# Routed attention and a cosine router: attention with keys on partitions and two heads per matmul slot

## The chip, the cores and the metric

One core of a Trainium2 chip runs the whole program. The metric is device time in microseconds of one execution. Before: 1521.6 us, the median of 3 runs (1513.58 to 1528.15).

## The reference

Attention runs on 4 batches, 8 heads, 768 tokens of 64 numbers. Each query and each key goes to the nearest of its head's 16 centroids by cosine, and a query sees only keys of its own cluster. The result, 3072 tokens of 512 numbers, goes through a router that sends each token to one of 8 experts.

```python
# attention: q, k, v (4, 8, 768, 64), centroids (8, 16, 64)
q_assign = argmax(einsum('bhsd,hcd->bhsc', q_n, c_n), axis=-1)      # *_n: rows of unit length
k_assign = argmax(einsum('bhsd,hcd->bhsc', k_n, c_n), axis=-1)
mask = q_assign[:, :, :, None] == k_assign[:, :, None, :]
scores = where(mask, scale * q @ k^T, -1e9)
scores = scores - max(scores, axis=-1)
attn = exp(scores);  attn = attn / (sum(attn, -1) + 1e-9)
x = attn @ v                                                        # to (3072, 512)
# router: 8 experts, 512 -> 1024 -> 512
idx, gate = argmax and softmax weight of cosine(x, expert_emb) / tau
out = gate * (relu(x @ w1[idx]) @ w2[idx])
```

All inputs and the output are fp32. A query without any key of its cluster has equal scores everywhere, so its row of x is the mean of v.

## The kernel before

The program has four stages in one stream: constants and a first preparation, attention with the routing of finished batches in between, the sorting of tokens by expert ("places"), and 31 blocks of 128 tokens through the experts. The change is in the first two.

Attention goes over 16 pairs of heads (4 batches with 4 pairs each). A pair has the two heads side by side: q and k are turned so that partitions 0 to 63 hold the numbers of the first head and 64 to 127 those of the second. A unit is one tile of 128 queries of one head, 6 tiles per head, 12 units per pair, 192 in all. Three units make a group, half a head, 64 groups in all.

What a unit does, by name and line:

- `scores` (L289): TensorE writes a 128 x 768 block, queries on partitions and all keys as columns, into two PSUM banks. Two bf16 matmuls (L296) multiply one-hot clusters so that keys of other clusters get a huge negative number; two fp32 matmuls, four instructions in the trace (L304), add q times k. Each uses the 64 partitions of its head. VectorE then finds the negated row maximum (L312).
- `expo` (L314): ScalarE takes the exponential with that maximum as bias and sums each row on the way (L320).
- `turn_probs` (L328): six TensorE transposes (L338) turn the probabilities so that keys lie on partitions; VectorE copies one half out of PSUM (L344), ScalarE the other (L346).
- `attend` (L349): for the group before, two key blocks per loop are multiplied with v into a 64 x 384 block (L356); after six blocks ScalarE copies it out (L365).
- `finish` (L367): for a group two back, three transposes (L373) turn the output, and VectorE divides by the row sums (L376, L377, L381) into `xr`, the rows of x of a batch.

Preparation of the next pair (`prep_pieces`, L200) is cut into nine pieces, one per loop: four times three transposes of q or k (L211) with a copy, the products with the centroids as 12 matmuls of 128 tokens against 32 columns (L227, `assign`), the choice of the first greatest product (VectorE and GpSimd), and the turning of the one-hot clusters (L259). Pieces, finish and routing share one PSUM bank, `misc`. Routing of a finished batch (`route_pieces`, L389) is cut into eight pieces in the same way.

The order on TensorE, VectorE and ScalarE is the written order of the main loop (L467): scores of unit i+1, finish, transposes of unit i, exponential of unit i+1, a piece of preparation, a third of attend, a piece of routing. Loads of q, k and v (`load`, L116) are issued on SyncE's queue and wait for a buffer, of which there are two of each.

Of the kernel before, what the change touches and what calls it, by code (L numbers as in the profile page):

```python
# [9 lines left out]
F32 = mybir.dt.float32  # L10
# [11 lines left out]
BIG = 2.0**60  # L22
# Adding and subtracting it rounds to an integer.
CMAGIC = 12582912.0
# Index of rows that hold no token: out of bounds, so they are not written.
# [8 lines left out]
def kernel(  # L34
# [31 lines left out]
    # Rows of x by token, each with the token's gate behind it.  # L66
# [13 lines left out]
    prefe = const.tile([P, E], BF16, name="prefe")  # L80
    io_i = const.tile([P, P], I32, name="io_i")
# [16 lines left out]
    # ================= attention and routing =================  # L98
    with ExitStack() as at:
# [39 lines left out]
        nc.vector.memset(onesb, 1.0)  # L139
        nc.vector.memset(cnB, 0.0)  # L140
# [9 lines left out]
        # Slot s = b * NJ + j holds token b * S + p * NJ + j on partition p.  # L150
# [10 lines left out]
        # One-hot clusters, 64 columns per head: those of the centroids, then -1 for q and 1 for k.  # L161
        ohs = [const.tile([P, 2, NJ, 2, D], BF16, name=f"oh{i}") for i in range(2)]
        for oh in ohs:
            nc.gpsimd.memset(oh, 0.0)
            for t in range(2):
                nc.gpsimd.memset(oh[:, t, :, :, C : C + 1], (-1.0, 1.0)[t])
# [33 lines left out]
        def prep_pieces(n):  # L200
            """Turned q (scaled) and k of a pair of heads, and their turned one-hot clusters."""
# [19 lines left out]

            def assign():
                bk = misc()
                for i, nm in enumerate("qk"):
                    for j in range(NJ):
                        c0 = 2 * C * (NJ * i + j)
                        nc.tensor.matmul(  # L227
                            bk[:, c0 : c0 + 2 * C],
                            lhsT=t[nm + "T"][:, P * j : P * j + P],
                            rhs=cnB[:, hp],  # L230
                            start=True,
                            stop=True,
                        )
# [9 lines left out]
            def choose():  # L243
                """One-hot clusters: the first of those with the greatest product."""
# [4 lines left out]
                    oh.rearrange("p t j h c -> p (t j h) c")[:, :, 0:C],  # L249
# [5 lines left out]
            def turn_hot(i, nm):  # L255
                hot = t[nm + "H"] = trp.tile([P, S], BF16, tag=nm + "H", name=nm + "H")
                bk = misc().bitcast(BF16)
                for j in range(NJ):
                    nc.tensor.transpose(  # L259
                        bk[:, P * j : P * j + P],  # L260
                        oh[:, i, j].rearrange("p h c -> p (h c)"),
# [6 lines left out]

            return [
                lambda: turn("q", 0),  # L270
                lambda: turn("k", 0),
                lambda: turn("q", 1),
                lambda: turn("k", 1),
                assign,
                None,
# [5 lines left out]
        # Units of attention: a tile of queries of one head; in groups of three, half a head.  # L281
        units = [(n, h, j) for n in range(len(pairs)) for h in range(2) for j in range(NJ)]
        GU = NJ // 2
# [5 lines left out]
        def scores(i):  # L289
            n, h, j = units[i]  # L290
            t = ld[n]
            rows = slice(D * h, D * h + D)
            s_ps = un[i]["s_ps"] = psS.tile([P, 1024], F32, tag="s_ps", name="s_ps")
            # The clusters first: between equal ones their sum is 0, and the scores stay exact.
            for lo, hi in ((0, 512), (512, S)):
                nc.tensor.matmul(  # L296
                    s_ps[:, lo:hi],
                    lhsT=t["qH"][rows, P * j : P * j + P],
                    rhs=t["kH"][rows, lo:hi],
                    start=True,  # L300
                    stop=False,
                )
            for lo, hi in ((0, 512), (512, S)):
                nc.tensor.matmul(  # L304
                    s_ps[:, lo:hi],
                    lhsT=t["qT"][rows, P * j : P * j + P],
                    rhs=t["kT"][rows, lo:hi],
                    start=False,
                    stop=True,
                )  # L310
            nmax = un[i]["nmax"] = smp.tile([P, 1], F32, tag="nmax", name="nmax", bufs=4)
            nc.vector.tensor_reduce(nmax, s_ps[:, 0:S], axis=AXX, op=ALU.max, negate=True)  # L312

        def expo(i):  # L314
            d = un[i]
            g, u = divmod(i, GU)
            if u == 0:
                gr[g]["den"] = smp.tile([P, GU], F32, tag="den", name="den", bufs=4)
            d["prob"] = pp.tile([P, S], F32, tag="prob", name="prob", bufs=3)
            nc.scalar.activation(  # L320
                d["prob"],
                d["s_ps"][:, 0:S],
                ACTF.Exp,
                bias=d["nmax"],
                accum_out=gr[g]["den"][:, u : u + 1],
            )

        def turn_probs(i):  # L328
            d = un[i]
            g, u = divmod(i, GU)  # L330
            if u == 0:
                gr[g]["pT"] = pp.tile([P, NJ, HS], F32, tag="pT", name="pT", bufs=2)
            pT = gr[g]["pT"]
            for half in range(2):
                t_ps = psT.tile([P, HS], F32, tag="t_ps", name="t_ps")
                for c in range(GU):
                    c0 = HS * half + P * c
                    nc.tensor.transpose(  # L338
                        t_ps[:, P * c : P * c + P], d["prob"][:, c0 : c0 + P], ident
                    )  # L340
                dst = pT[:, GU * half : GU * half + GU, P * u : P * u + P]
                src = t_ps.rearrange("p (c m) -> p c m", m=P)
                if half == 0:
                    nc.vector.tensor_copy(dst, src)  # L344
                else:
                    nc.scalar.copy(dst, src)  # L346
            d.clear()

        def attend(g, part):  # L349
# [405 lines left out]
```

## Time and profile before

| | |
|---|---|
| median of 3 runs | 1521.6 us (1513.58 to 1528.15) |
| span of the profiled execution | 1522.6 us |
| its own time beside the span | not given apart from the span |
| mean granted TensorE clock | 0.956 |
| busy: TensorE, VectorE, ScalarE, GpSimd | 1426.1, 469.1, 407.1, 117.0 us |

The span runs from the first to the last instruction of one execution. "Busy" is the time in which an engine works on an instruction; for TensorE, matmuls overlap in the records, so the time from one start to the next says more than a duration. A releaser in square brackets behind a row names what ended the engine's idle time before it. The granted clock is the share of full speed that TensorE was given; its levels are 1.2 and 2.4 GHz. In the first 50 us the column shows 1.00 although matmuls take twice their later time there. A timeline merges like instructions that follow each other; x4 is four of them.

### The profile page before, as it was taken

The numbers are of one execution on the slowest core, as the hardware profiler recorded it, in microseconds if no ns is written. First come the engines' busy times: TensorE is split into PE (matmuls) and PEld (weight loads), VectorE is DVE, ScalarE is ACT, GpSimd is POOL, SyncE is SP. The second block draws the span as 40 slices with busy tenths as digits, with TensorE's granted clock in tenths as the row PEclk, the third lists the DMA queues.
The fourth block names the chain that finished last, engine by engine and source line by source line (L and its number), as shares of the span: only waits on it lengthen the run. The fifth ranks groups of instructions, "written<-read, shape, count | busy, mean of one in ns | idle before, by whom it ended". The sixth has DMA issues, their size and how long they took to land.

```text
span 1522.6 us, 14912 instructions
## 1 busy us (share of the span) xinstructions
PE 1426.1 (94%) x5715; PEld 749.9 (49%) x5715; DVE 469.1 (31%) x925; ACT 407.1 (27%) x830; POOL 117.0 (8%) x153
## 2 busy tenths in 40 slices
PE   5999999989999998999998999957999999999997
PEld 3544554545455554555554555443444444444443
DVE  2434444333344333444443344432111111111110
ACT  2333333332333323333333333310111111111110
POOL 1000000000000010000000000021111111111110
PEclk9999999878999978999998999957999999999999
DMA  9110110101101101011011000000726575534310
GB/s 285 41 32 0 32 32 1 31 27 47 27 6 32 32 1 63 11 32 32 1 32 42 11 11 1 1 41 22 257 85 254 194 257 196 198 143 146 137 39 0
DMA packets 106134, 107.73 MB, mean 71 GB/s; under 512 B 77445, under 2 KB 77445, under 8 KB 105552
## 3 DMA queue, kind: packets, MB, share of 16 engines
q1 hardware_dynamic: 100928, 92.30, 19.0%
q0 software_dynamic: 4960, 14.44, 2.6%
q8 instruction: 45, 0.74, 0.2%
q14 instruction: 25, 0.20, 0.0%
q10 hardware_dynamic: 176, 0.05, 0.0%
HBM read 165.48 MB, written 14.43 MB: 118 GB/s over the span
## 4 chain that ended last, share of the span: by engine, by line
PE 60%; issue 20%; DMA 12%; DVE 4%; ACT 2%; POOL 0%; POOLq 0%; ACTq 0%; DVEq 0%
PE o_ps L356 19%; PE s_ps L304 17%; DMA out_dram<-y,sidx 12%; PE t_ps L338 9%; PE s_ps L296 6%; PE misc L227 3%; PE misc L211 2%; PE misc L411 2%; DVE nmax L312 2%; PE misc L401 1%; ACT xT L405 1%; PE misc L259 1%; DVE xr L381 1%; DVE den L377 0%; PE misc L373 0%
## 5 line engine op out<-in xcount | busy, mean ns | idle before, releaser
L312 DVE TENSOR_REDUCE nmax<-s_ps 128x1 f32<-128x768 f32 x192 | 183.8, 957 | 459.3 <-PE s_ps L304 459.3
L356 PE MATMUL o_ps<-pT,v 128*64 128x384 f32 x768 | 305.3, 523 | 0.0
L304 PE MATMUL s_ps<-kT,qT 64*128 64x512 f32 (+1 forms) x768 | 294.5, 506 | 0.0
L346 ACT COPY pT<-t_ps 128x384 f32<-128x384 f32 x192 | 91.7, 478 | 580.8 <-PE t_ps L338 580.8
L656 PE MATMUL h_ps<-w1s,xTm 128*128 128x512 f32 x496 | 222.2, 601 | 0.0
L679 PE MATMUL y_ps<-w2s,hT 128*128 128x512 f32 x496 | 218.7, 593 | 1.2 <-DVE hT L673 1.2
L304 PEld LDWEIGHTS s_ps<-kT,qT 64*128 64x128 f32 x768 | 135.1, 196 | 118.9 <-issue 95.4
L338 PE MATMUL t_ps<-ident,prob 128*128 128x128 f32 x1152 | 177.9, 293 | 0.0
L320 ACT ACTIVATE prob<-s_ps,nmax 128x768 f32<-128x768 f32 x192 | 173.9, 906 | 7.0 <-DVE den L376 3.7
L338 PEld LDWEIGHTS t_ps<-ident,prob 128*128 128x128 f32 x1152 | 130.2, 147 | 60.1 <-issue 57.4
L679 PEld LDWEIGHTS y_ps<-w2s,hT 128*128 128x128 f32 x496 | 93.9, 190 | 118.6 <-issue 116.7
L356 PEld LDWEIGHTS o_ps<-pT,v 128*64 128x64 f32 x768 | 93.6, 142 | 108.7 <-issue 104.9
L656 PEld LDWEIGHTS h_ps<-w1s,xTm 128*128 128x128 f32 x496 | 92.6, 191 | 110.2 <-issue 106.2
L648 DVE COPY xTm<-x_ps 128x512 f32<-128x512 f32 x31 | 21.4, 691 | 389.7 <-PE x_ps L646 389.7
L344 DVE COPY pT<-t_ps 128x384 f32<-128x384 f32 x192 | 105.2, 548 | 1.4 <-PE t_ps L338 1.3
L663 ACT ACTIVATE h<-h_ps 128x512 f32<-128x512 f32 x62 | 37.0, 597 | 248.0 <-PE h_ps L656 248.0
L296 PE MATMUL s_ps<-kH,qH 64*128 64x512 bf16 (+1 forms) x384 | 98.4, 337 | 0.9 <-ACT kH L267 0.9
L296 PEld LDWEIGHTS <-qH 64*128 64x128 bf16 x384 | 21.7, 95 | 105.5 <-issue 105.0
L687 ACT ACTIVATE y<-y_ps,xin 128x512 f32<-128x512 f32 x31 | 21.3, 687 | 188.1 <-PE y_ps L679 188.1
L241 POOL TENSOR_TENSOR sel<-sel,prefc 128x384 bf16<-128x384 bf16 x16 | 14.6, 911 | 639.4 <-DVE sel L240 639.4
L688 POOL DMA_INDIRECT out_dram<-y,sidx x31 | 31.4, 1014 | 410.2 <-ACT y L687 410.2
L673 DVE COPY hT<-r_ps 128x512 f32<-128x512 f32 x62 | 39.7, 681 | 26.7 <-PE r_ps L672 26.7
(138 smaller groups left out, 777.1 us busy)
## 6 DMA issues: line engine op xcount, KB each, us to landing
w1s<-in_moe_w_dram SPq DMA_DIRECT2D x33, 2048.0 KB
w2s<-in_moe_w_dram SPq DMA_DIRECT2D x33, 2048.0 KB
x_rows<-xr SPq DMA_DIRECT2D x4, 1539.0 KB
q<-in_q_dram SPq DMA_DIRECT2D x32, 192.0 KB
k<-in_k_dram SPq DMA_DIRECT2D x32, 192.0 KB
v<-in_v_dram SPq DMA_DIRECT2D x32, 192.0 KB
xin<-x_rows,gidx POOLq DMA_INDIRECT x31, 7.3
out_dram<-y,sidx POOLq DMA_INDIRECT x31, 7.5
```

The source lines that it names most:

```text
L227: nc.tensor.matmul(bk[:, c0 : c0 + 2 * C], lhsT=t[nm + "T"][:, P * j : P * j + P], rhs=cnB[:, hp], start=True, stop=True,)
L296: nc.tensor.matmul(s_ps[:, lo:hi], lhsT=t["qH"][rows, P * j : P * j + P], rhs=t["kH"][rows, lo:hi], start=True, stop=False,)
L304: nc.tensor.matmul(s_ps[:, lo:hi], lhsT=t["qT"][rows, P * j : P * j + P], rhs=t["kT"][rows, lo:hi], start=False, stop=True,)
L312: nc.vector.tensor_reduce(nmax, s_ps[:, 0:S], axis=AXX, op=ALU.max, negate=True)
L320: nc.scalar.activation(d["prob"], d["s_ps"][:, 0:S], ACTF.Exp, bias=d["nmax"], accum_out=gr[g]["den"][:, u : u + 1],)
L338: nc.tensor.transpose(t_ps[:, P * c : P * c + P], d["prob"][:, c0 : c0 + P], ident)
L344: nc.vector.tensor_copy(dst, src)
L346: nc.scalar.copy(dst, src)
L356: nc.tensor.matmul(d["o_ps"][:, 0:HS], lhsT=ld[n]["v"][:, c, h], rhs=d["pT"][:, c], start=(c == 0), stop=(c == NJ - 1),)
L656: nc.tensor.matmul(bk, lhsT=d["xT"][:, P * c : P * c + P], rhs=w1s[j % 2][:, c, f0 : f0 + 512], start=(c == 0), stop=(c == KD - 1),)
L673: nc.vector.tensor_copy(d["hT"][:, f0 : f0 + 512], bk)
L679: nc.tensor.matmul(bk, lhsT=d["hT"][:, P * c : P * c + P], rhs=w2s[j % 2][:, c], start=(c == 0), stop=(c == KF - 1),)
```

## The change

Scores are computed with keys on partitions: a unit is now a tile of 128 keys against 384 queries (half the queries) of both heads of a pair. Head 0 uses partitions 0 to 63 as operands and one PSUM bank, head 1 partitions 64 to 127 and another bank. There are again 12 units per pair and 192 in all; six of them make a group (`GU = NJ`), so 32 groups.

- The exponential of a unit is directly the moving operand of attend; the turning of probabilities with its copies is gone.
- There is no row maximum and no bias. Row sums are taken by VectorE, which adds the probabilities of the six key tiles into `acc`, and at the end by matmuls with a column of ones over partitions. A small constant (2^-100) added per key keeps rows without a key of their cluster at the mean of v: `values` sums v over tokens on GpSimd, `mean` multiplies by the constant, and `evict` adds it as a bias.
- `attend` writes head 0 to PSUM partitions 0 to 63 and head 1 to 64 to 127 of one bank, per unit two fp32 matmuls of 384 columns.
- The centroid products have the centroids as stationary operand: four matmuls, each to 32 PSUM partitions, of 384 columns (`products`), which are copied out and turned (`assign`). The one-hot tiles are laid out to match.
- PSUM: `psT` (two banks) is dropped; `o_ps` and `misc` get two banks each.
- The main loop emits scores and exponential of unit i+1, then evict or finish, a piece of preparation (ten pieces), attend of unit i, and a piece of routing.

```diff
-        psT = at.enter_context(tc.tile_pool(name="psT", bufs=2, space=PSUM))
-        psO = at.enter_context(tc.tile_pool(name="psO", bufs=1, space=PSUM))
-        psM = at.enter_context(tc.tile_pool(name="psM", bufs=1, space=PSUM))
+        psO = at.enter_context(tc.tile_pool(name="psO", bufs=2, space=PSUM))
+        psM = at.enter_context(tc.tile_pool(name="psM", bufs=2, space=PSUM))
...
+            def products():
+                bk = misc()
+                for i in range(4):
+                    nc.tensor.matmul(
+                        bk[2 * C * i : 2 * C * i + 2 * C, 0:HS],
+                        lhsT=cnB[:, hp],
+                        rhs=t["qk"[i // 2] + "T"][:, HS * (i % 2) : HS * (i % 2) + HS],
+                        start=True,
+                        stop=True,
+                    )
+                t["asT"] = smp.tile([P, HS], F32, tag="asT", name="asT")
+                nc.scalar.copy(t["asT"], bk[:, 0:HS])
+
             def assign():
                 bk = misc()
-                for i, nm in enumerate("qk"):
-                    for j in range(NJ):
...
+                for u in range(NJ // 2):
+                    nc.tensor.transpose(
+                        bk[:, P * u : P * u + P], t["asT"][:, P * u : P * u + P], ident
+                    )
...
+            def values():
+                v = t["v"]
+                vs = smp.tile([P, NJ // 2, 2, D], F32, tag="vs", name="vs")
+                nc.gpsimd.tensor_tensor(vs, v[:, 0 : NJ // 2], v[:, NJ // 2 :], ALU.add)
+                nc.gpsimd.tensor_tensor(vs[:, 0], vs[:, 0], vs[:, 1], ALU.add)
+                nc.gpsimd.tensor_tensor(vs[:, 0], vs[:, 0], vs[:, 2], ALU.add)
+                t["vs"] = vs
+
+            def mean():
+                bk = misc()
+                nc.tensor.matmul(bk[:, 0:1], lhsT=t["vs"][:, 0]..., rhs=epsc, start=True, stop=True)
+                t["ev"] = smp.tile([P, 1], F32, tag="ev", name="ev")
+                nc.vector.tensor_copy(t["ev"], bk[:, 0:1])
...
-        GU = NJ // 2
+        GU = NJ
+        units = [(n, hq, j) for n in range(len(pairs)) for hq in range(2) for j in range(NJ)]
...
+            s_ps = un[i]["s_ps"] = psS.tile([P, 2, 512], F32, tag="s_ps", name="s_ps")
+            for l, r, first in (("kH", "qH", True), ("kT", "qT", False)):
+                for h in range(2):
+                    rows = slice(D * h, D * h + D)
+                    nc.tensor.matmul(
+                        s_ps[:, h, 0:HS],
+                        lhsT=t[l][rows, P * j : P * j + P],
+                        rhs=t[r][rows, HS * hq : HS * hq + HS],
+                        start=first,
+                        stop=not first,
+                    )
 
         def expo(i):
             d = un[i]
+            d["prob"] = pp.tile([P, 2, HS], F32, tag="prob", name="prob", bufs=4)
+            nc.scalar.activation(d["prob"], d["s_ps"][:, :, 0:HS], ACTF.Exp)
+
+        def attend(i):
+            n, hq, j = units[i]
+            d, g = un[i], gr[i // GU]
+            if j == 0:
+                g["o_ps"] = psO.tile([P, 512], F32, tag="o_ps", name="o_ps")
+            for h in range(2):
+                nc.tensor.matmul(
+                    g["o_ps"][D * h : D * h + D, 0:HS],
+                    lhsT=ld[n]["v"][:, j, h],
+                    rhs=d["prob"][:, h],
+                    start=(j == 0),
+                    stop=(j == NJ - 1),
+                )
+            if j == 1:
+                g["acc"] = pp.tile([P, 2, HS], F32, tag="acc", name="acc")
+                nc.vector.scalar_tensor_tensor(
+                    out=g["acc"], in0=un[i - 1]["prob"], scalar=NJ * EPS, in1=d["prob"],
+                    op0=ALU.add, op1=ALU.add,
+                )
+                un[i - 1].clear()
+            elif j > 1:
+                nc.vector.tensor_tensor(g["acc"], g["acc"], d["prob"], ALU.add)
+                d.clear()
+
+        def evict(g):
+            n = units[GU * g][0]
             d = gr[g]
+            d["oT"] = smp.tile([P, HS], F32, tag="oT", name="oT")
+            nc.scalar.activation(d["oT"], d["o_ps"][:, 0:HS], ACTF.Identity, bias=ld[n]["ev"])
 
         def finish(g):
...
+            U = NJ // 2
             bk = misc()
+            for u in range(U):
+                for h in range(2):
+                    c0 = HS + 2 * u + h
+                    nc.tensor.matmul(
+                        bk[:, c0 : c0 + 1],
+                        lhsT=d["acc"][:, h, P * u : P * u + P],
+                        rhs=ones,
+                        start=True,
+                        stop=True,
+                    )
+            for u in range(U):
+                nc.tensor.transpose(bk[:, P * u : P * u + P], d["oT"][:, P * u : P * u + P], ident)
+            den = smp.tile([P, U, 2], F32, tag="den", name="den")
+            nc.vector.reciprocal(den.rearrange("p u h -> p (u h)"), bk[:, HS : HS + 2 * U])
...
                 if i + 1 < len(units):
                     scores(i + 1)
+                    expo(i + 1)
+                if part == 0 and g > 0:
+                    evict(g - 1)
+                if part == 1 and g > 0:
+                    finish(g - 1)
+                if prepare:
+                    prepare.pop(0)()
                 if i < len(units):
+                    attend(i)
                 if routing:
                     routing.pop(0)()
```

## Rows read from the trace of the kernel before

**Rows 1.** The page, busy us (share of the span) x instructions.

```profile
PE 1426.1 (94%) x5715; PEld 749.9 (49%) x5715; DVE 469.1 (31%) x925; ACT 407.1 (27%) x830; POOL 117.0 (8%) x153
```

**Rows 2.** Stretches: their length, each engine's busy us (instructions), clock, DMA share, GB/s.

```profile
400.00:600.00 200.00, 187.55 (x860) 102.12 (x859) 79.87 (x161) 68.68 (x145) 10.12 (x15) 0.93 0.10 26
1100.00:1522.00 422.00, 414.33 (x1193) 199.89 (x1191) 50.33 (x80) 51.48 (x82) 54.05 (x53) 0.99 0.42 152
```

**Rows 3.** Timeline of TensorE late in attention: start us, us, engine, line, operation, shapes, count.

```profile
959.58 1.50 PE L356 MATMUL o_ps<-pT,v 128*64 128x384 f32 x4
961.01 0.50 PE L296 MATMUL s_ps<-kH,qH 64*128 64x512 bf16 x2
961.35 1.45 PE L304 MATMUL s_ps<-kT,qT 64*128 64x512 f32 x4
962.73 0.88 PE L338 MATMUL t_ps<-ident,prob 128*128 128x128 f32 x6
963.54 1.50 PE L356 MATMUL o_ps<-pT,v 128*64 128x384 f32 x4
...
992.77 0.40 PE L373 MATMUL misc<-ident,oT 64*128 64x64 f32 x3 [0.62 <-ACT oT L365]
```

**Rows 4.** Chain of waits, cluster products of four pairs: start us, us, what.

```profile
276.65 2.60 PE misc L227 x24
...
365.75 2.60 PE misc L227 x24
...
420.41 2.60 PE misc L227 x24
...
475.07 2.60 PE misc L227 x24
```

**Rows 5.** Timeline of TensorE, output turns (L373) beside q-k passes (L304).

```profile
428.68 0.59 PE L304 MATMUL s_ps<-kT,qT 64*128 64x512 f32 x1
428.97 0.34 PE L373 MATMUL misc<-ident,oT 64*128 64x64 f32 x2
429.11 0.59 PE L304 MATMUL s_ps<-kT,qT 64*128 64x512 f32 x1
...
430.06 0.87 PE L338 MATMUL t_ps<-ident,prob 128*128 128x128 f32 x6
...
453.10 1.45 PE L304 MATMUL s_ps<-kT,qT 64*128 64x512 f32 x4
454.40 0.34 PE L373 MATMUL misc<-ident,oT 64*128 64x64 f32 x3
454.67 0.88 PE L338 MATMUL t_ps<-ident,prob 128*128 128x128 f32 x6
```

**Rows 6.** Groups: line, engine, operation, shapes, count | busy us, mean ns | idle before, releaser.

```profile
L312 DVE TENSOR_REDUCE nmax<-s_ps 128x1 f32<-128x768 f32 x192 | 183.8, 957 | 459.3 <-PE s_ps L304 459.3
L320 ACT ACTIVATE prob<-s_ps,nmax 128x768 f32<-128x768 f32 x192 | 173.9, 906 | 7.0 <-DVE den L376 3.7
L320 ACT ACTIVATION_READ_ACCUMULATOR prob<-s_ps,nmax 128x1 f32 x192 | 38.9, 202 | 0.0
L419 DVE TENSOR_REDUCE sq<-junk 128x1 f32<-128x512 f32 x24 | 16.2, 676 | 0.0
L398 POOL TENSOR_TENSOR junk<-xr 128x512 f32<-128x512 f32 x24 | 24.8, 1039 | 270.5 <-DVE sq L419 101.5 <-DVE xr L381 93.6 <-DVE den L376 75.3
```

**Rows 7.** Timeline of TensorE: a turn of q behind a finish.

```profile
456.42 0.55 PE L211 MATMUL misc<-ident,q 128*128 128x128 f32 x3 [0.88 <-DVE xr L381]
```

**Rows 8.** A stretch with routing, and a q-k part early in attention.

```profile
300.00:310.00 10.00, 9.27 (x40) 5.39 (x37) 2.74 (x6) 2.32 (x6) 1.04 (x1) 0.67 0.00 0
...
46.63 2.76 PE L304 MATMUL s_ps<-kT,qT 64*128 64x512 f32 x4
```

**Rows 9.** An issue of v, and a stretch of 1 us behind it.

```profile
412.35 1.23 SPq L122 DMA_DIRECT2D v<-in_v_dram  x2
...
416.00:417.00 1.00, 1.00 (x5) 0.54 (x6) 0.82 (x2) 0.43 (x2) 0.00 (x0) 1.00 0.05 8
```

More of the change, by code (lines that the diff above doesn't have):

```diff
@@ L22 @@
 BIG = 2.0**60
+EPS = 2.0**-100
 CMAGIC = 12582912.0
@@ L80 @@
     prefe = const.tile([P, E], BF16, name="prefe")
+    ones = const.tile([P, 1], F32, name="ones")
+    epsc = const.tile([P, 1], F32, name="epsc")
     io_i = const.tile([P, P], I32, name="io_i")
@@ L139 @@
         nc.vector.memset(onesb, 1.0)
+        nc.vector.memset(ones, 1.0)
+        nc.vector.memset(epsc, EPS)
         nc.vector.memset(cnB, 0.0)
@@ L160 @@
         nc.vector.tensor_scalar(tok_hi, tok_t, 1, None, ALU.add)
-        ohs = [const.tile([P, 2, NJ, 2, D], BF16, name=f"oh{i}") for i in range(2)]
+        ohs = [const.tile([P, NJ // 2, 4, 2, D], BF16, name=f"oh{i}") for i in range(2)]
         for oh in ohs:
@@ L273, in prep_pieces @@
                 lambda: turn("k", 1),
+                products,
                 assign,
-                None,
+                mean,
                 choose,
@@ L289, in scores @@
         def scores(i):
-            n, h, j = units[i]
+            n, hq, j = units[i]
             t = ld[n]
[L292 to L312, printed above, removed]
+            s_ps = un[i]["s_ps"] = psS.tile([P, 2, 512], F32, tag="s_ps", name="s_ps")
@@ L317, in expo @@
[L317 to L347, printed above, removed]
@@ L349, in attend @@
-        def attend(g, part):
-            n, h, _ = units[GU * g]
-            d = gr[g]
-            if part == 0:
-                d["o_ps"] = psO.tile([D, 512], F32, tag="o_ps", name="o_ps")
-            for c in range(2 * part, 2 * part + 2):
-                nc.tensor.matmul(
-                    d["o_ps"][:, 0:HS],
-                    lhsT=ld[n]["v"][:, c, h],
-                    rhs=d["pT"][:, c],
-                    start=(c == 0),
-                    stop=(c == NJ - 1),
-                )
-            if part == 2:
-                d["oT"] = smp.tile([D, HS], F32, tag="oT", name="oT")
-                nc.scalar.copy(d["oT"], d["o_ps"][:, 0:HS])
+            d["prob"] = pp.tile([P, 2, HS], F32, tag="prob", name="prob", bufs=4)
@@ new lines, in expo @@
+            nc.scalar.activation(d["prob"], d["s_ps"][:, :, 0:HS], ACTF.Exp)
+        def attend(i):
+            n, hq, j = units[i]
+            d, g = un[i], gr[i // GU]
[12 more added lines that the diff above has]
+                nc.vector.scalar_tensor_tensor(
+                    out=g["acc"],
+                    in0=un[i - 1]["prob"],
+                    scalar=NJ * EPS,
+                    in1=d["prob"],
+                    op0=ALU.add,
+                    op1=ALU.add,
+                )
[3 more added lines that the diff above has]
+                d.clear()
@@ L376, in finish @@
-            nc.vector.tensor_scalar(d["den"], d["den"], 1e-9, None, ALU.add)
-            nc.vector.reciprocal(d["den"], d["den"])
+            for u in range(U):
+                for h in range(2):
+                    c0 = HS + 2 * u + h
+                    nc.tensor.matmul(
+                        bk[:, c0 : c0 + 1],
+                        lhsT=d["acc"][:, h, P * u : P * u + P],
+                        rhs=ones,
+                        start=True,
+                        stop=True,
+                    )
@@ L466 @@
             expo(0)
-            for i in range(len(units) + GU):
+            for i in range(len(units) + 2):
+                g, part = divmod(i, GU)
                 if i < len(units) and i % (2 * NJ) == 0:
```

55 lines of the change are left out of this document (17 added, 38 removed).

## The prediction

> **What bounds the kernel now.** The page's busy line first: TensorE (PE) is busy for 94% of the span, VectorE (DVE) 31%, ScalarE (ACT) 27% [rows 1]. Then the table of stretches: from 400 to 600 us, inside attention, PE is busy 188 of 200 us and DVE and ACT 80 and 69; the expert blocks from 1100 us on are 414 of 422 us of PE [rows 2]. The change leaves those alone, so the question is what it does to PE's work in attention, whose last output turns start at 992.77 us [rows 3].
>
> The timeline of PE gives the price of one unit [rows 3]. From one start of the attend matmuls to the next is 963.54 - 959.58 = 3.96 us: attend 1.43 (to 961.01), scores 1.72 (cluster part 0.34, q-k part 1.38, to 962.73), transposes of the probabilities 0.81. Nothing stands between them: PE itself is the path. The chain of waits shows the pair: the cluster products of consecutive pairs start 54.66 us apart (475.07 - 420.41), and 12 units are 47.5 of that, so 7.1 us go to preparation, output turns and stalls [rows 4]. A pair with a batch's routing in it takes 365.75 - 276.65 = 89.1 us.
>
> Single passes come from the row with a finish in it. An fp32 matmul runs as two passes; a 512-column pass takes 429.11 - 428.68 = 0.43 us [rows 5], so a 384-column pass is 0.323. Four of those make 1.29, attend takes 1.43: 0.14 us is the switch to another shape. The four q-k passes (512, 512, 256, 256) make 1.29 of 1.38: 0.09 for that switch. 24 small instructions, each with a new weight load, take 2.60 us [rows 4]: 0.108 each.
>
> **Do halves of the array run side by side?** This decides most of the sum, and one row answers for row halves. In the second head of a pair, scores use partitions 64 to 127, and the output turns of L373 use 0 to 63. They are issued after all four q-k passes, yet they start at 428.97, between the first pass and the second, and the part still takes 430.06 - 428.68 = 1.38 us, as without them: they cost nothing [rows 3, 5]. In the first head both use partitions 0 to 63; there they come last and the part takes 454.67 - 453.10 = 1.57 us, 0.19 more [rows 5]. So work for another row half overtakes queued passes and overlaps them. For column halves (attend) no row exists. Bounds: none gained (1.29 us of passes) to all (0.645); I take all, since the row-half row is the nearest.
>
> The Trainium skill ("TensorE: Matmul & The Clock Gate", Part 3, The mechanism) says that matmuls start and end strictly in program order. By that rule the second pass of head 0 blocks the first of head 1, and each fp32 set takes three pass times of its four. The trace disagrees in the row-half case, as just read; the time by the rule is the rival "order kept". The same page (Measured speedup vs the span model) gives three column tiles 2.38 times one; an estimate at that efficiency, 79%, gives an attend some 0.17 us longer than full overlap. No trace here shows it.
>
> **The change, part by part, at the high clock.** There are again 192 units, now of 128 keys by 384 queries of two heads.
> - Transposes of probabilities: gone, 0.81 per unit, with the DVE and ACT copies behind them.
> - Scores: cluster part 0.165 (half of 0.33), q-k part 0.645, switch 0.09: 0.90. Attend: 0.645 + 0.14 = 0.79. The second half cannot start before its own weight load; I add 0.12 per stage, about one load at 0.108. Unit: 0.90 + 0.79 + 0.24 = 1.93 us. Bounds: 1.69 without that lag, 1.72 + 1.43 = 3.15 with no overlap.
> - Preparation per pair: turning q and k 12 x 0.108 = 1.3; cluster products, eight 384-column passes in column quarters, 2.6 in a row and 0.65 side by side, taken 0.8; their turns 3 x 0.108 = 0.3; mean 0.25; turned one-hots 12 x 0.108 = 1.3.
> - Finish, two per pair: the six sums over partitions are two instructions each with a full weight load, 12 x 0.108 = 1.3, and three turns 0.32: together 3.2.
> - Preparation now stands between scores and attend without transposes beside it: one more switch in 12 loops, 1.4.
> - Pair: 12 x 1.93 + 8.6 = 31.8 us against 54.66. Over 16 pairs this saves 16 x 22.9 = 366 us. The stalls of 0.88 us where a turn waits for the one "misc" bank [rows 7] are in the 54.66 and go with the second bank.
>
> **What must stay hidden.** ACT: exp takes 0.906 us [rows 6]; the 0.202 us read of its sum goes. From a scores end to its attend PE does one attend and one scores, 1.93 us; exp with some 0.25 us of hand-over needs 1.16. Without that cover each unit would wait up to 1.16. DVE: the maximum (0.957) and a copy go [rows 6]; five adds of 768 columns per six units come, each about 0.96 by the 676 ns of a 512-column reduction [rows 6] (estimate: scaled by columns and cut for the fixed part). With preparation about 1.2 us per unit, hidden under 1.93. Finish waits for the last add, one loop earlier. Evict goes into ACT's queue behind the next exp, and finish reads it a loop later. POOL: three adds of v per pair, at most 1.04 us each by a 512-column product [rows 6]. They wait for v, which is issued once the previous pair has released its buffer; there it landed from 412.35 to 416, 4 us [rows 9]. Behind them in POOL's queue stand the cluster selection and, in three pairs, routing's squares, for which a DVE reduction waits; the mean matmul comes six loops, some 16 us, later. Cost taken: none; bound 4 us in each of 16 pairs, 64 us. SP's loads keep their order.
>
> **Clock.** The granted clock is 0.67 in a stretch with routing [rows 8]: there small products with new weights and short waits stand among the units. At the low level (1.2 GHz) the q-k part takes 2.7 us, not 1.38 [rows 8]. The new finish has the same kind of small products. If its two loops per pair ran at 0.67, each some 4.2 us would grow by 2.1, over 32 loops 67 us; I take half, 33, and keep 0 and 67. The routing pairs' excess (34 us in the one shown) shrinks as passes do: I take 15 us in all, bounds 0 and 50. The start saves 3 us (two banks), the end 9 (no lag of a group; turns and logits of the last batch on two banks); both estimates, bounds 0 and 20 together.
>
> **Sum.** 1522.6 (span) - 366 - 15 - 12 + 33 = 1162.6, say 1162 us. The profiled execution's span is 1.0 us above the median of 1521.6; no separate time outside the span is shown, so the sum stands for the runs as it is.
>
> **Rivals.**
> - Row halves overlap, column halves don't: attend 1.43 for 0.91, cluster products 2.6 for 0.8: (0.52 x 12 + 1.8) x 16 = 129 more, about 1290. For: no row with column halves.
> - Order kept: three of four pass times: scores 0.165 + 0.97 + 0.09, attend 0.97 + 0.14, or 2.33 with no lag added: 0.40 x 192 = 77, and 13 for the products: 1252. Against: the output turns' overtaking [rows 5].
> - No overlap at all, or a compiled form that doesn't use halves: unit 3.15: (1.22 x 12 + 1.8) x 16 = 263 more: 1425.
> - Clock low: mean 0.67 throughout attention, as in the routing stretch: the 31.8 us of a pair become 47: 243 more, less the 33 already in: about 1375. Held at the low level all through, the unit's passes double (1.45 us more) and its small work nearly so: a pair near 55 us, about 1510, no gain. For: the q-k part at 46.63 us has no idle time ahead of it and is still at the low level [rows 8]. Against: the old units hold the high clock by their pass times at 428 to 454 us [rows 5], and the new ones keep both halves filled.
> - Slower: every change of half drains the array and exposes a load, side by side never. Place: four changes per unit (three in scores, one in attend). Price: a switch of 0.14 and an exposed load of 0.108, about 0.25 each. Unit 3.15 + 1.0 = 4.15; pair 12 x 4.15 + 10.4 = 60.2; 5.5 x 16 = 88 slower, with the other terms near 1615. It decides from 0.135 per change up, where the pair reaches 54.66. Against: the rows 5 turns, which cost nothing in the other half.
>
> **Chances.** Forecast 0.52, column halves serial 0.17, order kept 0.10, clock low 0.10, no overlap 0.07, slower 0.04. Forecast's own range: 1162 - 46 (no lag) - 33 = 1083 to 1162 + 34 + 32 (column efficiency left at the bound 0.17 per unit) = 1228. The range reaches over the next two rivals to 1320 and leaves out most of the clock case, no overlap and slower: about 2 in 10. About 1% is what can be told from no change: faster 0.94 (with a light clock case), within 1% 0.02, slower 0.04.
>
> **What would show it.** Row halves: q-k records of the two heads start within a weight load of each other, and scores to attend takes about 1.0 us. Column halves: the same for the attend records. Pair: cluster products some 32 us apart. Clock: granted clock by stretch, low beside finishes. Cover: PE idle before attend put down to exp, or before the mean put down to POOL. Wrong it would be if the unit is over 2.6 us at the high clock, if attention's mean clock is under 0.8, or if exp or the adds end last in each unit.

## The result and the profile after

| | median (lowest to highest), us | profiled execution: span | mean granted clock |
|---|---|---|---|
| before | 1524.88 (1513.58 to 1531.89) | 1522.6 | |
| changed | 1036.91 (1031.21 to 1039.25) | 1037.5 | 0.967 |

The changed kernel takes 0.679 of the time [0.675, 0.683]; the brackets hold a 95% interval. That is 488 us less. Where runs of one kernel lie more than 1.5% above its fastest, ratios and medians here leave them out. The prediction had the direction and most of the mechanism, but 1037 lies below the low end of its range, 1083.

The page of the changed kernel, busy us and share of the span. Against [rows 1] PE is busy for 441 us less, out of 485 us of span; its share has not fallen, so PE still sets the time.

```profile
PE 985.3 (95%) x4675; PEld 481.1 (46%) x4675; DVE 336.5 (32%) x591; ACT 290.9 (28%) x430; POOL 163.4 (16%) x201
```

The timeline of TensorE in attention: a finish, the cluster products of the next pair, and a plain unit (start us, us, engine, line, operation, shapes, count):

```profile
302.93 1.50 PE L390 MATMUL misc<-ones,acc 128*128 128x1 f32 x12
304.30 0.53 PE L398 MATMUL misc<-ident,oT 128*128 128x128 f32 x3
...
311.16 0.52 PE L231 MATMUL misc<-qT,cnB 128*32 128x384 f32 x2
311.17 0.52 PE L231 MATMUL misc<-kT,cnB 128*32 128x384 f32 x2
...
311.94 0.87 PE L353 MATMUL o_ps<-prob,v 128*64 128x384 f32 x4
...
326.78 0.34 PE L333 MATMUL s_ps<-qH,kH 64*128 64x384 bf16 x2
326.95 0.81 PE L333 MATMUL s_ps<-qT,kT 64*128 64x384 f32 x4
327.69 0.87 PE L353 MATMUL o_ps<-prob,v 128*64 128x384 f32 x4
328.49 0.34 PE L333 MATMUL s_ps<-qH,kH 64*128 64x384 bf16 x2
...
331.59 1.50 PE L390 MATMUL misc<-ones,acc 128*128 128x1 f32 x12
```

A unit is read from one cluster part to the next: 328.49 - 326.78 = 1.71 us, against 3.96 [rows 3]. It is scores 0.91 (0.17 and 0.74) and attend 0.80. Four 384-column passes of scores take 0.74, four of attend 0.80, where four in a row would take 1.29 and a switch of shape: two passes run at a time, in row halves and in column halves. The eight cluster passes in column quarters take 311.94 - 311.16 = 0.78 us. A pair is read from every second finish: 331.59 - 302.93 = 28.66 us, against 54.66 [rows 4].

The table of stretches, in the columns of [rows 2]: all of attention, 10 us with a finish in them, and the first and the third stretch with routing (the second, 270 to 300 us, reads like the first).

```profile
21.00:513.00 492.00, 483.68 (x3169) 229.97 (x3168) 253.27 (x414) 219.34 (x315) 80.24 (x95) 0.98 0.21 56
300.00:310.00 10.00, 10.00 (x67) 5.00 (x65) 5.02 (x7) 4.47 (x7) 2.50 (x3) 1.00 0.72 204
145.00:175.00 30.00, 28.48 (x206) 16.50 (x207) 16.96 (x41) 15.23 (x22) 7.55 (x11) 1.00 0.14 34
395.00:435.00 40.00, 39.44 (x237) 22.50 (x236) 17.84 (x41) 17.74 (x26) 7.55 (x11) 0.83 0.21 60
```

Two of the stretches with routing of the kernel before, the first and the third:

```profile
281.00:345.00 64.00, 57.23 (x224) 30.92 (x223) 21.44 (x52) 20.09 (x39) 5.82 (x11) 0.75 0.06 25
...
781.00:853.00 72.00, 64.03 (x292) 35.15 (x291) 27.34 (x63) 24.94 (x50) 6.25 (x11) 0.91 0.08 28
```

The granted clock of 1.00 is the 2.4 GHz level. Beside this finish it is 1.00, and in two of three routing stretches too; before, the two shown stand at 0.75 and 0.91, with PE idle for 6.8 and 8.0 us.

To compare clocks I cut attention, from 30 us on, into stretches of 5 us and add up 5 x (1 - granted clock): the time that a clock held at 1.00 would have saved PE. Before it is 41 us, in the changed kernel 6.8. All of the 6.8 lies in the third routing stretch, behind one of the 32 finishes; the attend after it takes 1.46 us to the next start, not 0.80:

```profile
410.60 1.50 PE L390 MATMUL misc<-ones,acc 128*128 128x1 f32 x12
...
412.42 1.54 PE L353 MATMUL o_ps<-prob,v 128*64 128x384 f32 x4
```

Not every execution has it: the run of 1031.21 us has a mean clock of 0.976 against the profiled one's 0.967, and experiment 1, which changes only an order, loses 0.8 us by this sum.

Where the 485.1 us between the two spans went:

| stage | before | changed | difference |
|---|---|---|---|
| start to the first scores | 27.2 | 20.4 | -6.8 |
| attention, to the first turn of the last routing | 966.4 | 492.7 | -473.7 |
| last routing, to the places | 26.2 | 20.4 | -5.8 |
| places | 20.5 | 20.5 | 0.0 |
| experts | 482.3 | 483.5 | +1.2 |

Attention's part splits into 16 pairs of 26.0 less (416), 48 less for the excess of the three pairs with routing (36.7 us over a plain pair in all, against 85.1), and some 9 in its first pair. The excess is read from the starts of the cluster products.

### The profile page after: what moved, and what is told of

Read it like the earlier page. It is cut to its first block, busy times and chain, and to the rows that moved or that the text cites. A ratio compares the mean times of both kernels' runs of the same rounds, so it can differ in the third digit from the quotient of the medians.

```text
span 1037.5 us, 11950 instructions
## 1 busy us (share of the span) xinstructions
PE 985.3 (95%) x4675; PEld 481.1 (46%) x4675; DVE 336.5 (32%) x591; ACT 290.9 (28%) x430; POOL 163.4 (16%) x201
## 4 chain that ended last, share of the span: by engine, by line
PE 45%; issue 30%; DMA 17%; DVE 5%; ACT 2%; POOL 0%; POOLq 0%; ACTq 0%; DVEq 0%
DMA out_dram<-y,sidx 17%; PE s_ps L333 15%; PE o_ps L353 13%; PE misc L390 4%; PE misc L216 3%; PE misc L436 3%; PE misc L426 2%; PE misc L273 1%; PE misc L231 1%; PE misc L398 1%; DVE oh L261 1%; DVE xr L404 1%; PE misc L244 1%; DVE pm L260 1%; DVE acc L372 1%
## 5 line engine op out<-in xcount | busy, mean ns | idle before, releaser
L344 ACT ACTIVATE prob<-s_ps 128x768 f32<-128x768 f32 x192 | 155.2, 810 | 249.0 <-PE s_ps L333 242.5
L353 PE MATMUL o_ps<-prob,v 128*64 128x384 f32 x768 | 168.3, 517 | 3.7 <-ACT prob L344 3.6
L333 PE MATMUL s_ps<-qT,kT 64*128 64x384 f32 x768 | 157.7, 489 | 0.0
L372 DVE TENSOR_TENSOR acc<-acc,prob 128x768 f32<-128x768 f32 x128 | 125.4, 979 | 17.6 <-ACT prob L344 11.3
L333 PEld LDWEIGHTS s_ps<-qT,kT 64*128 64x128 f32 x768 | 70.7, 194 | 0.5 <-issue 0.5
L333 PE MATMUL s_ps<-qH,kH 64*128 64x384 bf16 x384 | 65.2, 336 | 0.9 <-ACT kH L281 0.9
L353 PEld LDWEIGHTS o_ps<-prob,v 128*64 128x64 f32 x768 | 38.2, 135 | 54.2 <-issue 37.2
L390 PEld LDWEIGHTS misc<-ones,acc 128*128 128x128 f32 x384 | 45.3, 191 | 17.9 <-issue 15.3
L390 PE MATMUL misc<-ones,acc 128*128 128x1 f32 x384 | 48.0, 252 | 0.4 <-DVE acc L372 0.4
L423 POOL TENSOR_TENSOR junk<-xr 128x512 f32<-128x512 f32 x24 | 29.0, 1216 | 90.2 <-DVE sq L444 50.3
```

The source lines that it names most:

```text
L333: nc.tensor.matmul(s_ps[:, h, 0:HS], lhsT=t[l][rows, P * j : P * j + P], rhs=t[r][rows, HS * hq : HS * hq + HS], start=first, stop=not first,)
L344: nc.scalar.activation(d["prob"], d["s_ps"][:, :, 0:HS], ACTF.Exp)
L353: nc.tensor.matmul(g["o_ps"][D * h : D * h + D, 0:HS], lhsT=ld[n]["v"][:, j, h], rhs=d["prob"][:, h], start=(j == 0), stop=(j == NJ - 1),)
L372: nc.vector.tensor_tensor(g["acc"], g["acc"], d["prob"], ALU.add)
L390: nc.tensor.matmul(bk[:, c0 : c0 + 1], lhsT=d["acc"][:, h, P * u : P * u + P], rhs=ones, start=True, stop=True,)
```

## The experiments

Each is an edit of the changed kernel; the code lines are abridged. The question after the result: is the gain really the halves of the array (and which), and why does the clock stay up where it was expected to fall?

**1. Order of the scores (e_order).** The strict-order rival needs the second head's passes to stand behind the first's.

```
-for l, r, first in (("kH", "qH", True), ("kT", "qT", False)):
-    for h in range(2):
+for h in range(2):
+    for l, r, first in (("kH", "qH", True), ("kT", "qT", False)):
```

> The scores of a unit are issued head by head: cluster part and q-k part of head 0, then those of head 1. Theory (the two row halves have queues of their own, work of one overtakes queued work of the other): unit 1.71 us and the time 1037 us, both within 1% of the changed kernel. Rival (matmuls start strictly in program order, and the overlap comes from the written alternation of heads): head 1 begins only beside the last pass of head 0, scores take 0.16 + 4 x 0.32 + 0.09 = 1.5 us for 0.91, and 192 units add about 110 us: 1145 us.

Measured: 1035.47 us (1033.02 to 1039.97), ratio to the kernel before 0.681 [0.678, 0.685]. Timeline of TensorE:

```profile
325.77 0.34 PE L333 MATMUL s_ps<-qH,kH 64*128 64x384 bf16 x2
325.94 0.81 PE L333 MATMUL s_ps<-qT,kT 64*128 64x384 f32 x4
326.69 0.87 PE L353 MATMUL o_ps<-prob,v 128*64 128x384 f32 x4
327.48 0.34 PE L333 MATMUL s_ps<-qH,kH 64*128 64x384 bf16 x2
```

That the program took the new order shows in the weight loads (PEld), which now alternate between cluster and q-k part (in the changed kernel both cluster loads come first):

```profile
325.76 0.09 PEld L333 LDWEIGHTS <-kH 64*128 64x128 bf16 x1 [0.60 <-issue]
325.77 0.20 PEld L333 LDWEIGHTS s_ps<-qT,kT 64*128 64x128 f32 x1
325.77 0.09 PEld L333 LDWEIGHTS <-kH 64*128 64x128 bf16 x1
```

Issued wholly behind head 0, head 1 still shares its time: scores 0.92, unit 1.71. "Order kept" falls, for row halves; the order of attend's passes was not varied. The Trainium skill ("TensorE: Matmul & The Clock Gate", Part 3, The mechanism) states that matmuls start and end strictly in program order; the time of this run does not go by it, as the turns in [rows 5] did not.

**2. Attend in one column half (e_cols).** Both heads' attend passes write one column half (it alternates by group), so they cannot run side by side; the output is turned in six small pieces.

```
-g["o_ps"][D * h : D * h + D, 0:HS],
+o_all[c : c + D, h, 0:HS],          # c = D * (group % 2)
...
+for h in range(2): nc.scalar.activation(d["oT"][:, h], d["o_ps"][:, h, 0:HS], ...)
```

> Both heads of attend go to the same column half of the array (the half changes from group to group), two PSUM banks; the output turns become six small ones instead of three, and the mean is computed in both places. Scores keep their two row halves. Theory (column halves overlap fully): attend takes 1.43 us for 0.80, 0.63 x 192 = 121 us, and the small extras some 1 us a pair, 16 us: 1170 us. Rival (column halves give little, the gain over the forecast is in scores and in dropped copies): attend within 0.2 us of the changed kernel's and a time below 1095 us. Clock: if the granted clock is held by how full the array is, it falls in the routing stretches (below 0.85 there); if by the absence of waits, it stays near 1.00.

Measured: 1242.01 us (1236.01 to 1244.02), ratio 0.815 [0.811, 0.819]: over the expectation, because the edit added a wait of its own. PE's waits (us in all, times, longest), and then attention's stretch:

```profile
PE o_ps L357 <- ACT oT L385: 49.8, 31, 2.0
```

```profile
21.00:726.00 705.00, 653.46 (x3392) 307.81 (x3386) 253.94 (x420) 240.85 (x351) 80.47 (x97) 0.93 0.15 39
```

At each change of group the next attend waits up to 2.0 us for the copies out of the bank, and the clock of attention is 0.93, 44 us lost by the sum above. So the run was not the clean test it was meant to be.

**3. The same with the copies first (e_cols2).** The copies out of o_ps are issued ahead of the next scores and exp, so no attend waits for them.

```
+if part == 0 and g > 0: evict(g - 1)
 if i + 1 < len(units): scores(i + 1); expo(i + 1)
-if part == 0 and g > 0: evict(g - 1)
```

> As e_cols (both heads of attend in one column half), but the copies out of PSUM are issued ahead of the next scores and exponential, so that attend of the next group does not wait 1.6 us for them 31 times (49.8 us in e_cols). Theory (that wait, and the clock that fell behind it, are what e_cols cost beyond 1170 us): 1170 to 1190 us, no wait of TensorE for these copies above 0.4 us, and full clock outside routing. Rival (serial column halves cost more than their passes show): still above 1215 us.

Measured: 1153.51 us (1151.73 to 1155.03), ratio 0.757 [0.754, 0.760]; below the 1170 to 1190 expected.

```profile
401.33 1.50 PE L357 MATMUL o_ps<-prob,v 128*64 128x384 f32 x4
402.77 0.34 PE L336 MATMUL s_ps<-qH,kH 64*128 64x384 bf16 x2
402.94 0.81 PE L336 MATMUL s_ps<-qT,kT 64*128 64x384 f32 x4
403.68 1.18 PE L357 MATMUL o_ps<-prob,v 128*64 128x384 f32 x3
```

Attend is 1.44 us and scores still 0.91. Column halves are thus worth 117 us in all, by the unit (1.44 - 0.80) x 192 = 123. The other 88 us of experiment 2 are its 50 of waits and the clock behind them, where the lost time falls from 44 us to 2.

**4. One head per unit (e_onehead).** A unit is 128 keys of one head by all 768 queries: both scores passes in the same row half, both attend passes in the same column half. All transposes stay away and both misc banks stay. Two things move with it: `o_ps` is one tile of two banks, and a pair's two finishes stand in neighbouring loops, 5 to 7 us apart (14 to 21 in the changed kernel).

```
-units = [(n, hq, j) for n in range(len(pairs)) for hq in range(2) for j in range(NJ)]
+units = [(n, h, j) for n in range(len(pairs)) for h in range(2) for j in range(NJ)]
```

> Keys on partitions, no maximum and no turned probabilities, as in the changed kernel, but a unit is 128 keys of one head by all 768 queries: both matmuls of a kind use the same half of the array. The work in columns is the same. Theory: unit 1.72 + 1.43 = 3.15 us, 1.44 x 192 = 276 us more: 1315 us at the clock of the changed kernel. If the granted clock is held by a filled array, it is low early in attention and in the routing stretches as in the kernel before, and the time is 1340 us or more; if the second misc bank and its missing waits hold it, 1315 us and a clock of about 1.00 in the routing stretches. Rival (the halves matter little, dropping the transposes and copies gave the gain): below 1150 us.

Measured: 1328.13 us (1320.21 to 1333.21), ratio 0.873 [0.867, 0.878]. A unit late in attention, and a loop with a finish in it:

```profile
315.24 1.50 PE L391 MATMUL misc<-ones,acc 128*128 128x1 f32 x12
316.60 0.58 PE L399 MATMUL misc<-ident,oT 128*128 128x128 f32 x3
316.97 0.85 PE L216 MATMUL misc<-ident,k 128*128 128x128 f32 x3
317.74 2.78 PE L354 MATMUL o_ps<-prob,v 128*64 128x384 f32 x4
...
402.71 0.50 PE L334 MATMUL s_ps<-qH,kH 64*128 64x384 bf16 x2
403.04 1.45 PE L334 MATMUL s_ps<-qT,kT 64*128 64x384 f32 x4
404.42 1.50 PE L354 MATMUL o_ps<-prob,v 128*64 128x384 f32 x4
405.86 0.49 PE L334 MATMUL s_ps<-qH,kH 64*128 64x384 bf16 x2
```

Its stretches: attention up to 800 us, the finish just shown, and one with routing.

```profile
21.00:800.00 779.00, 779.00 (x3166) 377.40 (x3165) 248.88 (x414) 222.94 (x315) 74.20 (x94) 0.96 0.13 36
315.00:320.00 5.00, 5.00 (x23) 2.92 (x22) 2.08 (x4) 0.81 (x1) 1.67 (x3) 0.69 0.00 0
228.00:262.00 34.00, 34.00 (x172) 19.32 (x172) 14.40 (x30) 11.63 (x16) 6.51 (x9) 1.00 0.05 12
```

The unit is 3.15 us, the prediction's figure for no overlap; the halves together are worth 291 us, 276 of it by the unit ((3.15 - 1.71) x 192) and most of the rest clock. On the clock the run answers two ways. The routing stretch holds 1.00 with half of the array unused (as do the other two, 430 to 460 and 627 to 657 us), so filled halves are not needed for that. But behind a finish the clock falls with no idle moment ahead of it (attend 2.78 us for 1.50): below 0.9 in 20 of 154 stretches of 5 us, 27 us in all. The trace cut by 1 us has 16 such falls, each within 2 us of a finish's start. That is the loss that the prediction feared for the finish; the changed kernel has one such fall, 7 us.

The filled halves are the likely reason, but not shown apart. The two finishes close together don't explain five of the falls: they follow the first finish of a pair, as at 315.24, with 40 us since the one before, and the changed kernel runs the same row sums, output turns and turn of k at 302.93 us at 1.00. For the other 11 that is not ruled out. And column halves alone are not it: experiment 3 leaves half of the columns unused in attend, with its finishes where the changed kernel has them, and loses 2 us.

**5. One misc bank (e_misc1).** Only the second bank is taken back.

```
-psM = at.enter_context(tc.tile_pool(name="psM", bufs=2, space=PSUM))
+psM = at.enter_context(tc.tile_pool(name="psM", bufs=1, space=PSUM))
```

> The changed kernel with one misc bank instead of two, as in the kernel before. Theory (a filled array holds the clock): only the waits come back, 0.7 to 0.9 us in each routing loop and in the loops in which a turn follows a finish, 30 to 50 us in all: 1070 to 1085 us, clock in routing stretches as in the changed kernel. Rival (the waits made the clock fall): the clock is about 0.67 in the routing stretches, some 30 us more: 1100 us or above.

Measured: 1101.66 us (1099.37 to 1104.01; a fourth run took 1116.26), ratio 0.723 [0.719, 0.728]. PE's largest new waits (us in all, times, longest):

```profile
PE misc L436 <- ACT xT L430: 14.4, 20, 0.7
PE misc L216 <- PE misc L398: 13.0, 14, 0.9
```

Attention and two of its routing stretches:

```profile
21.00:572.00 551.00, 513.53 (x3183) 240.58 (x3183) 255.88 (x419) 220.94 (x316) 81.41 (x95) 0.94 0.20 51
157.00:192.00 35.00, 30.69 (x201) 16.99 (x201) 15.43 (x36) 13.01 (x19) 7.55 (x11) 0.95 0.10 24
300.00:338.00 38.00, 33.87 (x198) 19.66 (x198) 14.92 (x33) 12.42 (x19) 7.36 (x10) 0.82 0.10 22
```

The timeline of TensorE in the second of these:

```profile
310.95 0.87 PE L353 MATMUL o_ps<-prob,v 128*64 128x384 f32 x4
312.36 0.63 PE L426 MATMUL misc<-ident,xr 128*128 128x128 f32 x4 [0.54 <-DVE sel L253]
313.71 1.06 PE L436 MATMUL misc<-embT,xT 128*128 128x8 f32 x8 [0.73 <-ACT xT L430]
...
316.13 1.55 PE L353 MATMUL o_ps<-prob,v 128*64 128x384 f32 x4
```

65 us slower. Attention ends 59 us later: PE's idle time up to there grows from 8.3 to 37.5 (29), and its busy time from 483.7 to 513.5 (30) for the same matmuls. Most of the second part is clock (by the sum above 31 us lost, against 7): an attend of 0.87 us at 310.95 is one of 1.55 at 316.13, after a row of waits of 0.5 to 0.7 us. The last routing takes 27 us, against 20.4. The Trainium skill ("TensorE: Matmul & The Clock Gate", Part 1, A second HAM failure mode: psum-queue depth-cycling) describes a clock that swings because PE idles for moments between groups of matmuls as it cycles through PSUM banks. This trace agrees, with fp32 matmuls and waits of at most 1.5 us in this run's attention.

**6. One head and one bank (e_onehead_misc1).** The edits of 4 and 5 together: the new layout without its two companions.

> One head per unit (no half beside the other) and one misc bank: what is left of the change is keys on partitions, no maximum, no turned probabilities. Theory (waits at the misc bank and a half-filled array both pull the clock down, and together they do so most): some 30 us of waits and 30 to 50 us of lower clock over e_onehead's 1328 us: 1385 to 1410 us, routing stretches at a clock of about 0.7. Rival (only the waits count, the clock follows nothing else): 1358 us or less, routing stretches at about 0.9.

Measured: 1466.02 us (1465.80 to 1476.62; three more runs, the profiled one among them, took 1497.76 to 1511.54, so this kernel varies far more than the others), ratio 0.962 [0.957, 0.968]. Slower than either number expected. Attention in the profiled execution of 1497.76 us, beside the row of experiment 4:

```profile
27.00:960.00 933.00, 895.60 (x3136) 421.97 (x3136) 249.87 (x412) 221.76 (x312) 72.04 (x93) 0.85 0.10 28
```

Idle time is 37 us against none, busy time 117 more for the same matmuls. The four medians, 1037 and 1102 with halves, 1328 and 1466 without, make the second bank worth 65 us with halves and 138 without. The lost clock time of the four profiled executions is 7 and 31 with halves, 27 and 143 without. The 143 is from a long execution; by spans and mean clocks (0.885 over 1496 us there, 0.891 to 0.897 over 1464 to 1475 in the three shorter ones) an estimate for those is 120 to 130. So short waits alone or this half-used layout alone cost some 20 to 25 us, the two together over 110. The layout alone gains only 1522 - 1466 = 56 us, and 27 in the profiled execution: the transposes give 0.81 x 192 = 156, and the clock takes 143 - 41 = 102 of that back there. Why the two together cost so much more than their sum these runs do not settle.

**7. No adds (e_noadds).** Leaves out VectorE's adds of key tiles 2 to 5 into the row sums.

```
-nc.vector.tensor_tensor(g["acc"], g["acc"], d["prob"], ALU.add)
```

> The changed kernel without VectorE's adds of the key tiles 2 to 5 into the row sums (the sums cover only the first two tiles, so the division uses too small a number). Theory (the adds are hidden under TensorE): within 1% of 1037 us. Rival (VectorE's adds hold back the exponentials through the four probability buffers, or the finish): 15 us faster or more.

Measured: 1033.99 us (1031.05 to 1037.41), ratio 0.680 [0.676, 0.683]: no difference. These 128 adds, 125 us of VectorE in the changed kernel, are hidden.

**8 and 9. Sums by streaming (e_sums, e_sums2).** For a faster version: the finish loads 12 pieces of the sums as weights to stream one column each. Here ones are the weight and the sums are streamed, two heads in column halves; VectorE takes the reciprocal of 384 columns and scales before the turn. In e_sums the turns stand one loop later than these sums, in e_sums2 two.

```
-nc.tensor.matmul(bk[:, c0 : c0 + 1], lhsT=d["acc"][:, h, P * u : P * u + P], rhs=ones, ...)
+nc.tensor.matmul(bk[D * h : D * h + D, 0:HS], lhsT=ones, rhs=d["acc"][:, h], ...)
+nc.vector.reciprocal(rden, bk[:, 0:HS])
```

> The changed kernel with the sums over partitions turned round: ones (128 x 64) are the stationary operand and the row sums of 384 columns stream, each head in its column half, right behind attend; VectorE takes 384 reciprocals and scales the output before it is turned, and ScalarE copies the turned output out. 12 small instructions with full weight loads (1.30 us) become four passes in two halves (0.65 us) and one switch of shape goes (0.1): 0.7 x 32 = 24 us less, 1013 us. Rival (the reciprocal of 384 columns, by the rows of 3 and 6 columns about 2.5 us, fills VectorE and holds back the adds and the buffers of the exponential): no gain or slower than 1037 us.

Measured for e_sums: 1125.99 us (1119.25 to 1128.52), ratio 0.740 [0.737, 0.743]: 89 us slower than the changed kernel. The reciprocal in the table of groups, in the columns of [rows 6], and a turn behind it in TensorE's timeline:

```profile
L383 DVE RECIPROCAL rden<-misc 128x384 f32<-128x384 f32 x32 | 81.7, 2554 | 8.0 <-PE misc L379 7.8
```

```profile
314.40 0.87 PE L401 MATMUL misc<-ident,oT 128*128 128x128 f32 x3 [3.13 <-DVE oT L385]
...
315.84 1.55 PE L353 MATMUL o_ps<-prob,v 128*64 128x384 f32 x4
```

PE waits 77.5 us in 32 such waits, and passes after them run at the low level. PE's own work fell as meant (482.1 us busy in attention against 483.7, even with the lower clock).

> e_sums with the output turns two loops behind the row sums instead of one, so that TensorE does not wait 3.1 us for VectorE's reciprocal (2.55 us) and scaling; routing of a batch starts one loop later for it. Theory (e_sums lost by that wait and by the clock that fell behind it): no wait above 0.5 us before the turns, clock near 0.98 in attention, and the saving of e_sums comes out, 24 us: 1013 us. Rival (VectorE is too full with the reciprocals, 1.7 us of each 2.2 us loop, and holds back the copies of k or the exponential): 1037 us or more.

Measured for e_sums2: 1025.58 us (1024.78 to 1027.69), ratio 0.673 [0.670, 0.677], the fastest kernel here; against the changed kernel's 0.679 [0.675, 0.683] the intervals just overlap, so its 11 us are likely but not certain. The waits for oT fell to 15.5 us in 29 (the longest, 3.4, behind the last group), attention's clock is 0.98. The gain is about half of the 24 us expected.

## Why the prediction was wrong

Its likeliest case happened, and each rival fell: "column halves don't" and "no overlap" by the unit of 1.71 (experiments 3 and 4 show what they would have cost), "order kept" by experiment 1, "clock low" by attention's 0.98, "slower" by the same unit, which leaves no room for 0.25 us at a change of half. What failed are sizes, nearly all on one side:

| step | taken | measured | shift of the sum |
|---|---|---|---|
| "I add 0.12 per stage" of lag, 0.24 per unit | 46 | none; the unit is 1.71 for 1.93 | -42 |
| rest of a pair, 8.6 | 8.6 | 28.66 - 12 x 1.71 = 8.1 | -8 |
| clock beside the finish | +33 | 1.00 beside 31 of 32; the one fall, 7 us, is in a routing pair | -33 |
| excess of the routing pairs | -15 | -48 | -33 |
| start and end | -12 | -21, with 9 of the first pair | -9 |
| sum | 1162.6 | 1037.5 | -125 |

**The lag** was a guess that the second half's weight load stands exposed. The rows already spoke against it: the turns that overtook the q-k passes added nothing [rows 5], loads included. I took the row for the overlap and not for its price.

**The clock term did not come, and here a step of reasoning failed, not only a size.** I read the 0.67 of a routing stretch [rows 8] as the work of "small products with new weights and short waits", and carried it to the new finish. The mechanism exists: the clock falls behind half of experiment 4's finishes, and behind one in the changed kernel. But the finish of the changed kernel stands between passes that fill both halves, and has two banks, so it has neither the waits nor the half-used array. Experiments 4 to 6 show what losing these costs: 27, 31 and 143 us of clock, against 7. I had used the filled halves as an argument against the rival "clock low" and not in the term itself.

**The second bank was priced only as stalls inside the pair** that "go with the second bank" [rows 7]. It is worth 65 us at this overlap: 29 of waits up to the end of attention, some 24 of clock and 7 in the last routing (experiment 5). For the routing pairs I took 15 of bounds 0 to 50 and got the end. By the starts of the cluster products their excess was 85.1 us; it is some 56 with one bank (over a plain pair of 31.1), some 25 with two banks but no halves side by side (experiment 4), and 36.7 in the changed kernel. So it follows the bank; halves side by side are not needed for it. Each of the two stretches shown in experiment 5 holds 4 us of idle time, at a clock of 0.95 and 0.82. What else took the excess from 85.1 to 56 no run separates.

**What held.** The finish costs what was worked out (1.37 to its first turn, 1.3 taken). Exp (now 0.81 us) and the adds stay hidden (experiment 7), POOL's adds of v too: PE waits 3.6 us in all for exp, 0.4 for VectorE's adds, and no wait of it names the adds of v.

**The range** failed for the same reason. Its low end of 1083 put only the lag and the clock at their favourable ends. The routing excess at its own bound is 35 more, start and end 8 more, together 1040. The second bank helps all three (with one, the excess is 56 us, the first scores start at 24.8 us for 20.4, and the last routing takes 27 for 20.4), so they should have moved together. The 0.17 us per attend at the high end came in no run: attend is 0.80, where the sum for full overlap was 0.79.

## What to carry to other kernels

In these runs two 64-row or 64-column fp32 matmuls cost little more than one if they lie in different halves of the array (for row halves in either order of issue); price them at full overlap and no lag when the trace shows one overtaking. A low granted clock is to be read with the idle moments before it and with how much of the array the neighbouring passes use: a spare PSUM bank that removes waits of under a microsecond can be worth more than twice the waits. When a new layout brings such a spare with it, price the two apart, since the layout alone may give its gain back to the clock.

## What the runs showed of the hardware

- Short waits and the one-head layout, with half of the array unused, each lower the clock a little and together a lot: 7, 31, 27 and 143 us lost in the four profiled executions of experiment 6. Half of the columns unused in attend alone went with 2 us (experiment 3). No idle time is needed: in the changed kernel's third routing stretch PE is busy throughout until the clock has fallen.
- Eight fp32 passes of 384 columns in four column quarters take 0.78 us, 0.10 us a pass.
- VectorE's reciprocal of 384 columns takes 2.55 us, against 0.20 for the 6 columns of the finish: some 6.2 ns a column, which turned experiment 8 into a loss.
- VectorE's add of 768 columns takes 0.96 us in the median and up to 1.65 beside GpSimd's adds of v. In the timelines of VectorE and GpSimd:

```profile
307.08 1.65 DVE L372 TENSOR_TENSOR acc<-acc,prob 128x768 f32<-128x768 f32 x1
```

```profile
306.91 1.00 POOL L287 TENSOR_TENSOR vs<-v 128x384 f32<-128x384 f32 x1 [9.79 <-PE s_ps L333]
```

VectorE's adds, with two inputs from SBUF, slow GpSimd's squares in turn: 1039 ns in the mean before [rows 6], 1216 in the changed kernel, 1107 in experiment 7, which leaves four of five adds out. Experiment 7 gained no time by it.
